# First unit of a sparse attention and gated feed-forward kernel: pair 0 by the hardware DMA queue, key maxima from PSUM, turns a pair ahead, and unit 0's VectorE work spread over its steps

## Chip, core and metric

The kernel runs on one core of a Trainium2 chip. The metric is the time of one execution on the device in microseconds, the median over runs. Before the change it is 263.07 us over 8 runs (262.12 to 263.72).

The engines: TensorE (PE in the profile, its weight loads PEld), VectorE (DVE), ScalarE (ACT), GpSimd (POOL) and SyncE (SP). POOL and SP issue the DMAs here: POOL those that convert f32 to bf16 on the way, into a software queue; SP those of the hardware queue.

## The reference

Inputs are q, k, v of shape (4 batches, 8 heads, 768 tokens, 64) in f32, and weights of a gated feed-forward layer.

```python
k_sum = k.reshape(B, H, nb, 32, D).max(axis=3)      # maximum over blocks of 32 keys, nb = 24
v_sum = v.reshape(B, H, nb, 32, D).mean(axis=3)     # mean over blocks of 32 values
scores_l = scale * q @ k^T, kept where |i - j| < 16
scores_s = scale * q @ k_sum^T + log(32)
a = softmax over [scores_l, scores_s] together
attn = a @ [v ; v_sum]
x = attn as (B*S, H*D) = (3072, 512)
g, val = x @ w_gate, x @ w_val                      # 512 -> 1536
ffn_out = (gelu(g) * val) @ w_out                   # 1536 -> 512
out = x + sigmoid(x @ w_res) * ffn_out
```

## The kernel before

**Tiling.** The work is cut into 8 units of 384 tokens (`TU`), two for each batch. A unit has an attention part and a feed-forward part. Heads go in 4 pairs: the 64 dimensions of two heads fill the 128 partitions. Tokens go in tiles of 64 queries, 6 to a unit.

**Attention of a pair.** `kW` holds, for each tile of 64 queries, 128 columns: 16 keys before the tile, its own 64, 16 after, 24 block maxima and 8 zeros. So one matmul per tile and head gives a [128 x 64] block of scores, all that the softmax needs, with the keys on the partitions. In unit 0 two matmuls first write the mask (`nmask`, 0 or -30000) into the score bank, which the scores are added to (`mask_step`); in other units the exponentials are multiplied with the 0/1 mask afterwards (`mask_part`). ScalarE takes the exponential into `P`. `vext` holds the values of the same 96 tokens, the block means in the last 32 partitions, and a column of ones, so that `av_part` gives sums and normalizer in one matmul. In unit 0 the means' part is a second matmul from `vsum` (`blocks=True`), so that the rest needn't wait for it. `av_norm` divides on VectorE into `xn`; `xt_step` turns it by TensorE and copies it on ScalarE into `xT`.

**Making kW, qT and vext.** In batch 0 tokens are loaded with 96 partitions (`load_tokens`), turned by TensorE through the identity (`turn_pair`, in PSUM buffers `mm`), and copied: `k_step` copies the keys into `kW` on ScalarE (L199), and `k_rest` on VectorE takes block maxima from there (a maximum of halves, L206; a reduce, L208), the neighbours of each tile (L210, L211) and spreads the maxima over the tiles (L212). `q_step` copies on ScalarE (L216). Values are loaded in 7 chunks (`load_values`: six of 128 tokens, the first one with 112, and a last one of 16 tokens); `v_spread` copies between halves of the tiles on VectorE; `vsum_sum` makes block means by matmuls with `bmean`, one for each chunk; `vsum_out` copies them; `vsum_bc` writes them into `vext`.

**Feed-forward.** For each of 12 steps `fo`, 4 matmuls make g and 4 make vv (`half_fo`, 128x384 each), ScalarE takes Gelu (L370), VectorE multiplies (L371) into `gvT`. Then `res_part` and `ffn_step` give the output, finished by `end_step`.

**Order.** All orders are written out by hand in the program: each engine runs its instructions in the order of the calls. During the steps `fo` of one unit the values and keys of the next batch are prepared (`values_step`, `k_step`, `k_rest`, `q_step`), and at its end the next unit's attention is interleaved with its `ffn_step`. `keep_warm(n)` puts n matmuls on zeros into TensorE's queue; there are 30 in the first unit.

**Loads.** On POOL, in this order: k and q of pairs 0 and 1, then of pairs 2 and 3 (between them the `affine_select` that makes the identity), value chunks 0 to 6 with the selects of the mask and of `bmean` between them, six pairs of weight chunks (columns for two steps fo each), q of unit 1 (`qb`), `w_res`, three chunks of `w_out`, then batch 1 (`load_batch`, called at fo 4 of unit 0). A load is given one of eight semaphores in turn, so that a load's issue waits for the landing of the eighth load before it.

The stretch ahead of unit 0's steps, and the functions that the change touches:

Of the kernel before, what the change touches and what calls it, by code (L numbers as in the profile page):

```python
# [15 lines left out]
def kernel(  # L16
# [86 lines left out]
    with tc.manual_schedule():  # L103
# [13 lines left out]
        def select(ap, op, fill, base, step, cm):  # L117
            nc.gpsimd.affine_select(out=ap, in_=ap, compare_op=op, fill=fill, base=base,
                                    pattern=[[step, ap.shape[-1]]], channel_multiplier=cm)

        def mask_consts():
            nc.vector.memset(maskt[:], 1.0)
            select(maskt[0:96], ALU.is_ge, 0.0, -1, -1, 1)
            select(maskt[0:96], ALU.is_ge, 0.0, 2 * WIN - 1, 1, -1)
            nc.vector.tensor_scalar(nmask[:], maskt[:], 30000.0, -30000.0, ALU.mult, ALU.add)

        nc.vector.memset(warm[:], 0.0)
        nc.vector.memset(ident[:], 0.0)
        nc.vector.memset(bias_t[:], 0.0)
        nc.vector.memset(bias_t[96:128, :], logblk)  # L130
        nc.vector.memset(bmean[:], 1.0 / BLK)
        vext_consts(0)

        kt, qa, qb = token_tile(0, S, "k0"), token_tile(0, TU, "qa"), token_tile(TU, S, "qb")
        k_sb[0] = kt
        load_tokens(kt, k, 0, 0, S, 0, 4)
        select(ident[:], ALU.not_equal, 1.0, 0, -1, 1)
        load_tokens(qa, q, 0, 0, TU, 0, 4)
        load_tokens(kt, k, 0, 0, S, 4, 8)
        load_tokens(qa, q, 0, 0, TU, 4, 8)  # L140
        select(bias_t[96:128, :], ALU.is_ge, -30000.0, NB - 1, 0, -1)
        load_values(0, 0)
        mask_consts()
        kw_consts(0)
        load_values(0, 1)
        select(bmean[:], ALU.is_ge, 0.0, 32 * (NB + 94) - WIN, -32, 1)
        select(bmean[:], ALU.is_ge, 0.0, 31 + WIN - 32 * (NB + 94), 32, -1)
        for c in range(2, NC + 1):
            load_values(0, c)
        nc.vector.memset(vsum[0][96:128, :, D:D + 1], 1.0)  # L150

        wg_src = moe_w_gate.rearrange("(ko ki) f -> ki ko f", ki=128)
        wv_src = moe_w_val.rearrange("(ko ki) f -> ki ko f", ki=128)
        for c in range(6):
            sl = slice(c * 256, (c + 1) * 256)
            nc.gpsimd.dma_start(out=w_gate[:, :, sl], in_=wg_src[:, :, sl])
            nc.gpsimd.dma_start(out=w_val[:, :, sl], in_=wv_src[:, :, sl])
        load_tokens(qb, q, 0, TU, S, 0, H)
        nc.gpsimd.dma_start(out=w_res[:], in_=moe_w_res.rearrange("(ko ki) f -> ki ko f", ki=128))
# [53 lines left out]

        def q_step(src, b, lo, hi, hp, pool, tag):
            tp = turn_pair(src, hp, pool, tag)
            nc.scalar.copy(qT[b % 2][hp][:, lo:hi].rearrange("d (p j) -> d p j", j=tp.shape[2]), tp)  # L216

# [29 lines left out]

        def vsum_sum(b, pool, tag, chunks=range(NC + 1), vs=None):
            if vs is None:
                vs = pool.tile([128, DM], F32, tag=tag, name="vs")  # L250
            for c in chunks:
                lo = NB - 2 - 4 * c if c < NC else 0
                rows, t = (slice(0, 128), 2 * c) if c < NC else (slice(64, 64 + WIN), NT - 1)
                nc.tensor.matmul(vs[:], bmean[rows, lo:lo + 128], vext[b % 2][rows, t, :, 0:D],  # L254
                                 start=(c == 0), stop=(c == NC), skip_group_check=True)
            return vs

        def vsum_out(b, vs, h0, h1, copy):
            copy(vsum[b % 2][96:128, h0:h1, 0:D],
                 vs[96:128, h0 * D:h1 * D].rearrange("p (h d) -> p h d", d=D))  # L260
# [14 lines left out]

        def mask_step():
            s = ps_s.tile([128, 2, 512], F32, tag="s", name="s")
            for hh in range(2):
                nc.tensor.matmul(s[:, hh, 0:TU].rearrange("p (t q) -> p t q", t=HT), ident[:],
                                 nmask.unsqueeze(1).to_broadcast([128, HT, QT]),  # L280
                                 start=True, stop=False, skip_group_check=True)
            return s

        def s_step(u, hp, st, s=None, two=None, masked=True):
            b, half = u // 2, u % 2
            first = s is not None
            if two:
                s = [pool.tile([128, 512], F32, tag=tag, name="s1") for pool, tag in two]
            elif not first:
                s = ps_s.tile([128, 2, 512], F32, tag="s", name="s")  # L290
# [126 lines left out]
        def values_step(u, fo):  # L417

            b = u // 2 + 1
            if u == 1 and fo >= 8:  # L420
                i = fo - 8
                if i == 0:
                    vs = vsum_sum(1, *SS)
                    vsum_out(1, vs, 0, H, nc.scalar.copy)
                    v_spread(1, 0, HT // 2, 0)
                if i == 1:
                    v_spread(1, 0, HT // 2, 1)
                if i in (2, 3):
                    vsum_bc(1, 2 * i - 4, 0, HT)
                    vsum_bc(1, 2 * i - 3, 0, HT)  # L430
            if u in (2, 4) and fo >= FO - NP:
                block_sums(vT[b], fo - FO + NP)
            if u in (3, 5):
                if fo in (1, 3):
                    v_spread(b, 0, HT // 2, fo // 2)
                if fo == 4:
                    vsum_turn(b, *SS)
                if 5 <= fo < 9:
                    vsum_bc(b, fo - 5, 0, HT)
            if u % 2 == 0 and u < NU - 1:  # L440
                if fo in (0, 1):
                    v_spread(b - 1, HT // 2, NC, fo)
                if fo in (2, 3):
                    vsum_bc(b - 1, 2 * fo - 4, HT, NT)
                    vsum_bc(b - 1, 2 * fo - 3, HT, NT)


        st = new_unit()
        wp = ps_o.tile([128, 512], F32, tag="ao", name="wp")
        keep_warm(13, wp)  # L450
        nc.scalar.activation(pre[:], bias_t[0:1, :], AF.Exp)
        for hp in range(2):
            k_step(0, hp, *MM)
            q_step(qa, 0, 0, TU, hp, *MM)
        s = mask_step()
        keep_warm(3, wp)
        s_step(0, 0, st, s)
        k_step(0, 2, *MM)
        q_step(qa, 0, 0, TU, 2, *MM)
        s = mask_step()  # L460
        s_step(0, 1, st, s)
        k_step(0, 3, *MM)
        q_step(qa, 0, 0, TU, 3, *MM)
        s = mask_step()
        s_step(0, 2, st, s)
        v_spread(0, 0, HT // 2, 0)
        v_spread(0, 0, HT // 2, 1)
        vs = vsum_sum(0, *MM, range(0, 3))
        keep_warm(2, wp)
        s = mask_step()  # L470
        s_step(0, 3, st, s)
        keep_warm(2, wp)
        for c in range(3, NC + 1):
            vsum_sum(0, *MM, range(c, c + 1), vs)
            keep_warm(2 if c < NC else 1, wp)
        vsum_out(0, vs, 0, 2, nc.vector.tensor_copy)
        vsum_out(0, vs, 2, 8, nc.scalar.copy)
        nc.scalar.activation(pre[:], bias_t[0:1, :], AF.Gelu)
        homes = (AO, TT, MM, MM)
        for p in (0, 2):  # L480
            for hp in (p, p + 1):
                av_part(0, hp, st, *homes[hp], blocks=False)
            for hp in (p, p + 1):
                av_part(0, hp, st, blocks=True)
                av_norm(hp, st)
        keep_warm(3)
        two = ps_s.tile([128, 2, 512], F32, tag="s", name="gv0")
        firsts = [(w_gate, 0, two[:, 0, :]), (w_val, 0, two[:, 1, :]), (w_gate, 1, None), (w_val, 1, None)]
        for hp in range(NP):
            xt_step(0, hp, st, *(TT if hp % 2 else AO), nc.scalar.copy)  # L490
            if hp:
                firsts = [(w, fo, half_fo(st, w, fo, hp - 1, hp, acc)) for w, fo, acc in firsts]

        for u in range(NU):
# [17 lines left out]
            for fo in range(FO):  # L512
# [11 lines left out]
                if u == 0 and fo == 4:  # L524
                    nc.vector.memset(vsT[:], 0.0)
                    vext_consts(1)
                    kw_consts(1)
                    load_batch(1)
                if u == 2 and fo == FO - 1:
# [9 lines left out]
                if u == 1 and fo == 6:  # L539
                    gate(gvT[0:1, fo, 0:1])  # L540
                    load_batch(2)
                if u == 1 and fo in (0, 1, 4, 5):
                    home = TT if fo % 2 else AO
                    if fo < 4:
                        k_step(nb, fo, *home)
                    else:
                        q_step(q_sb[nb], nb, 0, S, fo - 4, *home)
                if u == 1 and fo >= FO - 2:
                    k_rest(kW[1][fo - FO + NP])
                if u == 0 and fo >= FO - 2:  # L550
                    for hp in range(2 * (fo - FO + 2), 2 * (fo - FO + 2) + 2):
                        q_step(qb, 0, TU, S, hp, *(TT if hp % 2 else AO))
# [108 lines left out]
```

## Time and profile before

The profiled execution took 263.07 us, its span (first to last instruction) is 260.8 us.

| what | value |
|---|---|
| TensorE busy | 250.6 us, 96% of the span |
| VectorE, ScalarE busy | 173.4 us (66%), 130.3 us (50%) |
| g and vv matmuls (L364) | 712 listed, 0.326 us each, pipelined at about 0.16 |
| Gelu (L370), gvT product (L371) | 0.49 us, 0.55 us |
| exponential of a pair (L305) or half (L302) | 0.90 us, 0.58 us |
| kW copy (L199), qT copy of 384 (L216) | 0.80 us, 0.49 us |
| halves' maximum (L206), reduce (L208) | 0.35 us, 0.55 us |
| value chunk issue on POOL (L99) | 0.89 us |
| DMA | 29.6 MB, 113 GB/s on average, 190 to 205 GB/s in most of the first 45 us |

The page lists instructions by engine and line, with the tile written and the tiles read; a row's last part says how long its engine sat idle before it and what ended that. The granted clock is that of TensorE's throttle. A matmul's duration in a row includes the pipeline, so that the distance between starts, not the duration, is what a queue of them costs.

### The profile page before, as it was taken

How to read it: one execution, taken by the hardware profiler on the slowest of the kernel's cores; microseconds unless marked ns; L12 is line 12 of the kernel's file. 1: busy time of each engine (PE TensorE's matmuls, PEld its weight loads, DVE VectorE, ACT ScalarE, POOL GpSimd, SP SyncE). 2: the span in 40 equal slices, each digit the busy share in tenths (PEclk: the TensorE clock that was granted, in tenths of full speed). 3: DMA queues.
4: the chain of work that ended last, by engine and by line, in shares of the span. 5: the costliest groups of instructions: out<-in, count | busy, mean ns of one | idle time of the engine just before them, and what ended most of it. 6: DMA issues, size and time to landing. Idle time of an engine off the chain costs nothing.

```text
span 260.8 us, 5738 instructions
## 1 busy us (share of the span) xinstructions
PE 250.6 (96%) x2239; PEld 140.7 (54%) x2264; DVE 173.4 (66%) x414; ACT 130.3 (50%) x224; POOL 100.3 (38%) x137
## 2 busy tenths in 40 slices
PE   7789999999999999999999999999999999999995
PEld 2536554556555565555555565455645565556544
DVE  3744862576497878679966778588948754674424
ACT  2745449556375535745374535735364536443310
POOL 7966542990899910997560100010000100020000
PEclk9999999999999999999999999999999999999999
DMA  5999999999999999999993885644002200130012
GB/s 80 173 168 196 196 205 193 143 153 187 150 122 129 166 157 160 110 175 205 157 138 36 197 124 91 48 127 87 0 4 74 95 0 0 33 112 26 1 40 80
DMA packets 116746, 29.60 MB, mean 113 GB/s; under 512 B 103664, under 2 KB 114544, under 8 KB 116720
## 3 DMA queue, kind: packets, MB, share of 16 engines
q0 software_dynamic: 86992, 19.41, 84.2%
q1 hardware_dynamic: 29728, 9.84, 22.0%
q8 instruction: 17, 0.28, 0.5%
q14 instruction: 9, 0.07, 0.1%
HBM read 32.51 MB, written 6.29 MB: 149 GB/s over the span
## 4 chain that ended last, share of the span: by engine, by line
PE 84%; DVE 6%; POOL 3%; DMA 3%; issue 2%; ACT 1%; POOLq 0%; DVEq 0%
PE f L398 22%; PE vv L364 21%; PE g L364 20%; PE r L382 8%; PE ao L328 4%; DMA vext<-in_v_dram 3%; PE gv L510 3%; PE s L296 2%; DVE gvT L371 2%; POOL vext L99 2%; PE xp L347 1%; PE vs L254 1%; DVE ks L208 1%; DVE vext L274 1%; PE gv L364 1%
## 5 line engine op out<-in xcount | busy, mean ns | idle before, releaser
L364 PE MATMUL vv<-xT,w_val 128*128 128x384 bf16 x364 | 74.5, 326 | 0.2 <-DVE gvT L371 0.2
L370 ACT ACTIVATE ge<-g 128x384 f32<-128x384 f32 x87 | 42.7, 490 | 61.8 <-PE g L364 33.8
L364 PE MATMUL g<-xT,w_gate 128*128 128x384 bf16 x348 | 71.3, 326 | 0.0
L371 DVE TENSOR_TENSOR gvT<-ge,vv 128x384 bf16<-128x384 f32 x91 | 49.8, 551 | 27.9 <-PE vv L364 26.0
L398 PE MATMUL f<-w_out,gvT 128*128 128x512 bf16 (+2 forms) x298 | 66.6, 362 | 0.7
L364 PEld LDWEIGHTS <-w_val 128*128 128x128 bf16 x368 | 36.0, 98 | 24.8 <-issue 1.2
L364 PEld LDWEIGHTS <-w_gate 128*128 128x128 bf16 x352 | 33.9, 98 | 22.7 <-issue 0.7
L398 PEld LDWEIGHTS <-gvT 128*128 128x128 bf16 x312 | 28.3, 98 | 28.2
L409 POOL DMA_DIRECT2D out_dram<-o x12 | 6.5, 544 | 92.6 <-DVE rz L336 77.7
L388 ACT ACTIVATE th<-r 128x512 f32<-128x512 f32 x24 | 14.2, 602 | 25.9 <-PE r L382 25.9
L403 DVE SCALAR_TENSOR_TENSOR th<-th,f 128x512 f32<-128x512 f32 (+2 forms) x26 | 16.7, 641 | 12.3 <-PE f L398 8.5
L382 PE MATMUL r<-w_res,xT 128*128 128x512 bf16 x88 | 24.0, 380 | 0.4
L99 POOL DMA_DIRECT2D vext<-in_v_dram x28 | 23.6, 886 | 1.4 <-PE g L364 0.7
L313 DVE TENSOR_TENSOR P<-P,maskt 128x768 bf16<-128x768 bf16 x28 | 15.5, 557 | 12.5 <-ACT P L305 8.3
L172 POOL DMA_DIRECT2D k_sb<-in_k_dram x24 | 19.7, 848 | 10.2 <-DMA w_out<-in_moe_w_out_dram 5.2
L172 POOL DMA_DIRECT2D q_sb<-in_q_dram x24 | 20.0, 873 | 0.0
L338 DVE TENSOR_TENSOR xn<-ao,rz 128x384 bf16<-128x384 f32 x32 | 17.8, 557 | 1.1
L305 ACT ACTIVATE P<-s,bias_t 128x768 bf16<-128x768 f32 x18 | 16.2, 902 | 3.8 <-PE s L296 3.7
L349 ACT COPY xT<-xp 128x384 bf16<-128x384 bf16 x20 | 9.3, 480 | 17.5 <-PE xp L347 15.8
L405 DVE SCALAR_TENSOR_TENSOR o<-th,xn 128x512 f32<-128x512 f32 (+2 forms) x26 | 16.9, 651 | 0.9
L302 ACT ACTIVATE P<-s,bias_t 128x384 bf16<-128x384 f32 x28 | 14.6, 577 | 0.0
L172 POOL DMA_DIRECT2D v_sb<-in_v_dram x16 | 13.2, 866 | 2.9 <-DMA q_sb<-in_q_dram 2.9
(87 smaller groups left out, 230.7 us busy)
## 6 DMA issues: line engine op xcount, KB each, us to landing
out_dram<-o POOLq DMA_DIRECT2D x12, 256.0 KB, 2.4
out_dram<-o SPq DMA_DIRECT2D x11, 256.0 KB, 5.3
vext<-in_v_dram POOLq DMA_DIRECT2D x20, 128.0 KB, 6.9
k_sb<-in_k_dram POOLq DMA_DIRECT2D x24, 96.0 KB, 5.4
q_sb<-in_q_dram POOLq DMA_DIRECT2D x24, 96.0 KB, 4.3
w_gate<-in_moe_w_gate_dram POOLq DMA_DIRECT2D x6, 256.0 KB, 8.7
w_val<-in_moe_w_val_dram POOLq DMA_DIRECT2D x6, 256.0 KB, 8.9
w_out<-in_moe_w_out_dram POOLq DMA_DIRECT2D x3, 512.0 KB, 14.1
```

What stands on the lines that cost most here:

```text
L99: nc.gpsimd.dma_start(out=dst, in_=v[b, :, lo:hi, :].rearrange("h p d -> p h d"))
L172: nc.gpsimd.dma_start(out=sb[b][:, h // 2, :, h % 2 * D:h % 2 * D + D], in_=src[b, h].rearrange("(c p) d -> p c d", c=NC))
L305: nc.scalar.activation(P.rearrange("p a t q -> p a (t q)"), s[:, :, 0:TU], AF.Exp, scale=scale, bias=bias_t[:])
L313: nc.vector.tensor_mul(Pf, Pf, maskt.unsqueeze(1).to_broadcast([128, 2 * HT, QT]))
L338: nc.vector.tensor_mul(xn, ao[:, :, :, 0:D], rz.to_broadcast([128, NSUB, 2, D]))
L364: nc.tensor.matmul(acc[:, 0:TU], w[:, ko, fs], st["xT"][:, ko, :], start=(ko == 0), stop=(ko == KO - 1))
L370: nc.scalar.activation(ge[:], g[:, 0:TU], AF.Gelu)
L371: nc.vector.tensor_mul(gvT[:, fo, :], ge[:], vv[:, 0:TU])
L382: nc.tensor.matmul(r[:], st["xT"][:, ko, ss], w_res[:, ko, :], start=(ko == 0), stop=(ko == KO - 1))
L398: nc.tensor.matmul(st["f", sub][:, 0:c1 - c0], gvT[:, fo, ss], w_out[:, fo, c0:c1], start=(fo == 0), stop=(fo == FO - 1))
L403: nc.vector.scalar_tensor_tensor(th, th, 1.0, f[:, 0:c1 - c0], ALU.add, ALU.mult)
L405: nc.vector.scalar_tensor_tensor(o[:, 0:c1 - c0].rearrange("p (k d) -> p k d", d=128), th.rearrange("p (k d) -> p k d", d=128), 0.5, st["x ...
```

## The change

It rewrites the stretch ahead of unit 0's steps and moves work in units 0 and 1. The k and q of pair 0 come by SP as f32 (`kf`, `qf`) and are converted on ScalarE and VectorE; POOL loads the other pairs one by one. The 16-token value chunk is loaded first, the constants are made in another order, and `qb` is loaded before the last pair of weight chunks. In unit 0 `k_first` and `k_first_rest` take block maxima by one reduce out of PSUM and fill only the tiles of unit 0; `k_later` fills those of unit 1 in steps 8 to 11. Keys and queries of a pair are turned before the scores of the pair before it; pairs 1 and 3 have their scores in two single banks. The matmuls of `av_part` without block means stand ahead of the last sums of means; Gelu's table is loaded after the last exponential. 18 matmuls on zeros are left of 30.

```diff
@@ loads and constants
-        load_tokens(kt, k, 0, 0, S, 0, 4)
+        kf = qk.tile([PP, 2, 8 * D], F32, tag="k_sb", name="kf")
+        qf = qk.tile([PP, 2, 4 * D], F32, tag="q_sb", name="qf")
+        nc.sync.dma_start(out=kf[:], in_=k[0, 0:2].rearrange("h (p j) d -> p h (j d)", j=8))
+        nc.sync.dma_start(out=qf[:], in_=q[0, 0:2, 0:TU].rearrange("h (p j) d -> p h (j d)", j=4))
+        load_tokens(kt, k, 0, 0, S, 2, 4)
         select(ident[:], ALU.not_equal, 1.0, 0, -1, 1)
-        load_tokens(qa, q, 0, 0, TU, 0, 4)
-        load_tokens(kt, k, 0, 0, S, 4, 8)
-        load_tokens(qa, q, 0, 0, TU, 4, 8)
+        load_tokens(qa, q, 0, 0, TU, 2, 4)
+        for h in (4, 6):
+            load_tokens(kt, k, 0, 0, S, h, h + 2)
+            load_tokens(qa, q, 0, 0, TU, h, h + 2)
+        select(maskt[0:96], ALU.is_ge, 0.0, -1, -1, 1)
+        select(maskt[0:96], ALU.is_ge, 0.0, 2 * WIN - 1, 1, -1)
+        load_values(0, NC)
+        load_values(0, 0)
         select(bias_t[96:128, :], ALU.is_ge, -30000.0, NB - 1, 0, -1)
...
+        for c in range(1, NC):
+            load_values(0, c)
         select(bmean[:], ALU.is_ge, 0.0, 32 * (NB + 94) - WIN, -32, 1)
         select(bmean[:], ALU.is_ge, 0.0, 31 + WIN - 32 * (NB + 94), 32, -1)
...
         for c in range(6):
             sl = slice(c * 256, (c + 1) * 256)
+            if c == 5:
+                load_tokens(qb, q, 0, TU, S, 0, H)
...
@@ keys of unit 0
+        def k_first(hp):
+            tp = ps_mm.tile([128, 8, PP], BF16, tag="mm", name="tp")
+            for j in range(8):
+                for hh in range(2):
+                    nc.tensor.transpose(tp[hh * 64:hh * 64 + 64, j, :], kt[:, 2 * hp + hh, j, :], ident[0:PP, 0:PP])
+            kw = kW[0][hp]
+            nc.scalar.copy(kw[:, :, OWN:OWN + QT].rearrange("d t (p j) -> d t p j", j=8),
+                           tp.rearrange("d j (t p) -> d t p j", t=NT))
+            return tp, kw
+
+        def k_first_rest(tp, kw):
+            ks = work.tile([128, NB], BF16, tag="ks", name="ks")
+            nc.vector.tensor_reduce(out=ks[:], in_=tp.rearrange("d j (n w) -> d n j w", w=4),
+                                    axis=mybir.AxisListType.XY, op=ALU.max)
+            nc.vector.tensor_copy(kw[:, 0:HT, BLK0:BLK0 + NB], ks.unsqueeze(1).to_broadcast([128, HT, NB]))
+            nc.vector.tensor_copy(kw[:, 1:HT, 0:WIN], kw[:, 0:HT - 1, OWN + QT - WIN:OWN + QT])
+            nc.vector.tensor_copy(kw[:, 0:HT, POST:POST + WIN], kw[:, 1:HT + 1, OWN:OWN + WIN])
+
+        def k_later(kw):
+            nc.vector.tensor_copy(kw[:, HT:NT, 0:WIN], kw[:, HT - 1:NT - 1, OWN + QT - WIN:OWN + QT])
+            nc.vector.tensor_copy(kw[:, HT:NT - 1, POST:POST + WIN], kw[:, HT + 1:NT, OWN:OWN + WIN])
+            nc.vector.tensor_copy(kw[:, HT:NT, BLK0:BLK0 + NB], kw[:, 0:HT, BLK0:BLK0 + NB])
@@ the stretch ahead of unit 0's steps
+        s1 = s_tiles((AO, TT))
+        keep_warm(8, s1[0])
+        nc.scalar.copy(kt[:, 0].rearrange("p j d -> p (j d)"), kf[:, 0])
+        nc.vector.tensor_copy(kt[:, 1].rearrange("p j d -> p (j d)"), kf[:, 1])
+        nc.vector.tensor_copy(qa[:, 0:2].rearrange("p h j d -> p h (j d)"), qf[:])
+        t = k_first(0)
+        q_step(qa, 0, 0, TU, 0, *MM, nc.vector.tensor_copy)
+        nc.vector.tensor_scalar(nmask[:], maskt[:], 30000.0, -30000.0, ALU.mult, ALU.add)
+        k_first_rest(*t)
+        t = k_first(1)
+        q_step(qa, 0, 0, TU, 1, *MM)
+        k_first_rest(*t)
+        s = mask_into(s_tiles())
+        keep_warm(2, s1[0])
+        s_step(0, 0, st, s)
+        keep_warm(2, s1[0])
+        mask_into(s1)
+        t = k_first(2)
+        q_step(qa, 0, 0, TU, 2, *MM)
+        k_first_rest(*t)
+        s_step(0, 1, st, s1, True)
+        s = mask_into(s_tiles())
+        t = k_first(3)
+        q_step(qa, 0, 0, TU, 3, *MM, nc.vector.tensor_copy)
+        k_first_rest(*t)
+        vs = ps_mm.tile([128, DM], F32, tag="mm", name="vs")
+        keep_warm(1, vs)
+        s_step(0, 2, st, s)
+        s3 = mask_into(s_tiles((AO, TT)))
+        wp = ps_mm.tile([128, 512], F32, tag="mm", name="wp")
+        vsum_sum(0, *MM, (NC, 0), vs)
+        keep_warm(2, wp)
+        s_step(0, 3, st, s3, True)
+        nc.scalar.activation(pre[:], bias_t[0:1, :], AF.Gelu)
         v_spread(0, 0, HT // 2, 0)
         v_spread(0, 0, HT // 2, 1)
-        vs = vsum_sum(0, *MM, range(0, 3))
+        vsum_sum(0, *MM, (1, 2, 3), vs, first=False)
         keep_warm(2, wp)
...
+        homes = (MM, MM, AO, TT)
+        for hp in range(2):
+            av_part(0, hp, st, *homes[hp], blocks=False)
+        vsum_sum(0, *MM, (4,), vs, first=False)
+        for hp in range(2, NP):
+            av_part(0, hp, st, *homes[hp], blocks=False)
+        keep_warm(1, wp)
+        vsum_sum(0, *MM, (5,), vs, first=False, last=True)
         vsum_out(0, vs, 0, 2, nc.vector.tensor_copy)
         vsum_out(0, vs, 2, 8, nc.scalar.copy)
+        for hp in range(NP):
+            av_part(0, hp, st, blocks=True)
+            av_norm(hp, st)
-        keep_warm(3)
...
@@ units 0 and 1
-                if fo in (2, 3):
-                    vsum_bc(b - 1, 2 * fo - 4, HT, NT)
-                    vsum_bc(b - 1, 2 * fo - 3, HT, NT)
+                if 2 <= fo < 2 + NP:
+                    vsum_bc(b - 1, fo - 2, HT, NT)
...
                 if u == 0 and fo == 4:
                     nc.vector.memset(vsT[:], 0.0)
+                    load_rows(1)
+                if u == 0 and fo == 6:
                     vext_consts(1)
+                if u == 0 and fo == FO - 1:
                     kw_consts(1)
-                    load_batch(1)
+                    for c in range(NC + 1):
+                        load_values(1, c)
-                if u == 1 and fo in (0, 1, 4, 5):
+                if u == 1 and fo in (1, 2, 6, 7):
...
-                if u == 1 and fo >= FO - 2:
-                    k_rest(kW[1][fo - FO + NP])
-                if u == 0 and fo >= FO - 2:
-                    for hp in range(2 * (fo - FO + 2), 2 * (fo - FO + 2) + 2):
+                if u == 1 and fo in (8, 9):
+                    k_rest(kW[1][fo - 6])
+                if u == 0 and fo >= FO - 4:
+                    k_later(kW[0][fo - FO + 4])
+                if u == 0 and fo in (FO - 3, FO - 2):
+                    for hp in range(2 * (fo - FO + 3), 2 * (fo - FO + 3) + 2):
```

In unit 1's `values_step`, the sums of block means (`vsum_sum`, `vsum_out`) and the first `v_spread` move from fo 8 to fo 10, and the second `v_spread` and all four `vsum_bc` to fo 11.

## The prediction

> **What bounds the kernel now.** I read the windows table first, then the chain of waits, then the timeline of the stretches that these single out. Columns of the windows: stretch, its length, busy time of each engine with its count of instructions, granted clock, DMA share, GB/s.
>
> ```profile
> 5.00:10.00 5.00, 3.65 (x71) 2.04 (x71) 3.12 (x21) 2.36 (x4) 4.81 (x9) 1.00 1.32 191
> 10.00:15.00 5.00, 3.87 (x82) 2.41 (x82) 3.03 (x13) 4.65 (x7) 4.75 (x7) 1.00 2.89 150
> 15.00:20.00 5.00, 4.45 (x33) 1.69 (x33) 1.94 (x6) 1.08 (x3) 2.87 (x4) 1.00 1.78 180
> 20.00:25.00 5.00, 4.44 (x117) 3.43 (x118) 2.73 (x8) 3.20 (x6) 3.47 (x6) 1.00 1.45 197
> 25.00:30.00 5.00, 5.00 (x34) 3.03 (x33) 2.97 (x6) 2.40 (x6) 2.85 (x5) 1.00 1.45 196
> ```
>
> From 25 us on TensorE is full, and the page has it 96% busy over 260.8 us. So a gain must come from the first 25 us, or from a stall later. Much of the early busy time is warm-up matmuls on zeros. The chain in that window names what really ends last:
>
> ```profile
> 6.17 0.83 POOL vext L99
> 7.71 2.57 POOL vext L99 x3
> 10.27 8.09 DMA vext<-in_v_dram
> 19.91 2.07 PE ao L328 x96
> ```
>
> The value chunk issued at 9.4 lands at 17.4, the next at 18.4; until then nothing that needs the block means can start. The timeline shows what follows:
>
> ```profile
> 18.40 0.38 PE L254 MATMUL vs<-vext,bmean 128*128 128x512 bf16 x1 [0.16 <-DMA vext<-in_v_dram]
> ...
> 19.47 0.39 PE L415 MATMUL wp<-warm 128*128 128x512 bf16 x1
> 19.91 0.57 PE L328 MATMUL ao<-vext,P 96*64 96x65 bf16 x24
> ```
>
> All 96 ao matmuls queue behind the last vs sum, so the first reciprocal comes at 20.83, then four norms at 0.69 each:
>
> ```profile
> 20.83 0.20 DVE L336 RECIPROCAL rz<-ao 128x6 f32<-128x6 f32 x1 [0.96 <-PE ao L328]
> ...
> 23.14 0.56 DVE L338 TENSOR_TENSOR xn<-ao,rz 128x384 bf16<-128x384 f32 x1
> ```
>
> The last quarter of fo 0 then starts at 25.83, and full feed-forward work at 26.5. Two later stalls:
>
> ```profile
> 41.71 0.33 PE L296 MATMUL s<-qT,kW 64*128 64x64 bf16 x11 [0.20 <-ACT qT L216]
> ...
> 78.89 0.85 PE L328 MATMUL ao<-vext,P 128*64 128x65 bf16 x24 [0.24 <-DVE P L313]
> ```
>
> At unit 0's end the 24 score matmuls took 40.86 to 41.98, 1.12 us; at unit 1's end 73.70 to 74.16, 0.46. The difference, 0.66, is the late q copies. At 78.48 the r matmuls end, ao starts at 78.89 and takes 0.78 where 0.50 is usual: 0.69 lost to late masks.
>
> **The change, step by step (us after the span's start).**
>
> *Pair 0 by the hardware queue.* SP is free at 0.8, so kf is issued at about 0.9, qf 0.3 later (an SP issue takes 0.33). The nearest row is SP's output writes: 1.6 to landing at best, and 256 KB alone moved in 0.85 after 0.9 of latency. kf (384 KB in f32) then lands near 3.2, qf near 3.7. Bounds: 2.5, and 5.9 if it took the 5.0 that the first k load by POOL took. Up to 4.1 it costs nothing: VectorE's constants end at 3.59 now, plus twelve kW memsets (0.4, as at 34.3) gives 4.1. Then its two casts; no row shows an f32 cast from SBUF; between 0.30 (32x128 cast) and 0.70 (64x1536 copy) I take 0.45: 5.0. ScalarE's cast (0.60, as the 128x512 tanh) is beside it. TensorE is in its 8 warm-up matmuls (0.43 each) until 4.7.
>
> *Pair 0 to scores.* k turns (0.53) to 5.25, q turns (0.36) to 5.6, kW copy on ScalarE (0.80) to 6.05, qT copy on VectorE to 6.1. Here stands a new wait: nmask now queues on VectorE behind these and ahead of the maxima, and waits for maskt, whose selects stand on POOL behind six token loads (about 0.6 to 0.7 each from 1.4): 6.2. With nmask (0.78 before) 6.9. The maxima: one 128x768 reduce (0.95, as the vsT reduce) to 7.9, three copies 0.5 to 8.4. Scores at 8.45, against 9.68 now.
>
> *Pairs 1 to 3.* The maxima read PSUM, but in the changed program the reduce still waits for ScalarE's copy of the same tile. So ScalarE's order rules: P0 8.85 to 9.75, kW2 to 10.95, qT2 to 11.45, P1 as two halves (2 x 0.52) to 12.5, kW3 13.3; reduce and copies to 14.75; scores 3 at 14.8, P3 done at 16.25 (now 16.85). k and q of pair 3, last landing at 11.2 now, come in a queue relieved of pair 0's 288 KB (1.5 us at the 191 GB/s of the window): 10, in time for the turns at 11.
>
> *Values.* v_spread runs 14.75 to 16.15 on VectorE (0.70 each), then ao without blocks for pairs 0 and 1, vs 4, pairs 2 and 3, a warm-up, vs 5: 17.9. The last value chunk is issued near 11.3 and, without the two to three us [...], lands near 14.5; with that lag 17: either way in time. vsum 18.25, blocks, first reciprocal near 18.6 (now 20.83). VectorE's norms end at 21.5; turns, copies and first quarters fit between, no three warm-up matmuls stand ahead, and fo 0's last quarter starts at 22.4 instead of 25.83: 3.4 gained. Gelu's table load (1.28) moves to 16.3 to 17.6, covered by the vs sums; were they earlier it would hold vsum's copy, at most 1.
>
> *Unit 0.* k_later's twelve copies (about 0.15 each), vsum_bc singly and the constants at fo 4, 6, 11 keep gvT in step: the bunched memsets at 32.3 to 34.6 now cost 0.26 (nine steps of 1.30 from 26.48 make fo 9 35.58; it starts at 35.84). qb is turned a step earlier: 0.66. Unit 1: k_rest a step or two earlier, vs at fo 10: VectorE gets vs's 1.7 to catch up, masks end before r does: 0.65.
>
> *What the weight stream allows.* Weights are issued after bmean, near 12.9, data from 14.5; at 1.32 per 256 KB (the spacing of landings now) and qb (2.0) ahead of chunk 5, its w_val lands between 32.7 and 34.9. It is needed at 37.79 less 3.7 plus the moved q turns, 34.6: nothing to 0.3. Batch 1's last values land at 67.3 now, 0.7 before vs; the stream gains some 1.0, vs moves to 67.96 + 2.6 - 4.3 = 66.3: up to 0.5 lost, I take 0.3.
>
> *Two rules against this change.* (1) L211 took 0.60 and L212 0.56 at 8.9, where POOL was issuing:
>
> ```profile
> 8.86 0.60 DVE L211 COPY kW<-kW 128x176 bf16<-128x176 bf16 x1
> ...
> 10.41 0.19 DVE L211 COPY kW<-kW 128x176 bf16<-128x176 bf16 x1
> ```
>
> The Trainium skill, "GPSIMD Engine Reference", Key points, says that GpSimd shares its SBUF interfaces with VectorE and that VectorE's two-port modes contend. POOL now issues without pause to 12.9. By the rule each pair's copies pay 0.4, of which two pairs lie on the path: gain 0.8 less. By the row, two of four copies under POOL paid nothing; I take 0.2. (2) The warm-up: loads of warm come each 0.43 to 4.66, then four in 0.75, so the array went to full speed after 3.4 us of matmuls. The skill, "TensorE: Matmul & The Clock Gate", Part 1, says that the window is free-running and that an idle window halves the clock. 8 matmuls last just 3.4. By the rule the release may slip past 4.7; the granted clock of 1.00 in every window says that it doesn't here. Price below.
>
> Sum: 3.4 + 0.26 + 0.66 + 0.65 = 5.0, less 0.2 (contention) and 0.3 (batch 1's values): 4.5. The profiled execution is 263.07 (span 260.8, 2.3 around it), which is the median of the eight runs: 258.6.
>
> **Rivals.**
> - *The DMA stream takes it back.* The weights' head start is only about 1 us, since POOL issues them later. If one engine lags longer, chunk 5 or batch 1's values stop TensorE until the stream comes: with their slack now (4.0 less 2.0 for qb plus 0.5; 0.7 plus 2.6 for the two moved steps), the gain ends near 2 to 3: 260.6. For: the DMA is saturated to 67 us. Against: all weights have 4 us in hand now.
> - *The front is no faster.* Casts, nmask and ScalarE's order are all new waits ahead of v_spread; if they add 3 us (a late kf, 5.9, adds 1.8; contention 1.2), norms start as now and only the later stalls are won: 1.2 less 0.5, 262.3, hardly the same.
> - *Slower: the clock gate.* Twelve of 30 warm-up matmuls go (18 stay), and the turns that fill the front may not count: the same page, Part 4, says so of transposes. No row here shows it. If the array is at half clock from 5 us and released only by unit 0's dense work, its part of the front's path (some 4 us) doubles and 3.4 to 6.8 us of unit 0 run at half speed, 1.7 to 3.4 lost: 6 to 7 against 4.5, 265. It decides from 4.5 us lost, that is if the release comes after about 23 us.
>
> **How the numbers follow.** 0.3% (0.8 us) is about what a measurement of this kernel can tell from no change. Main case 0.66 (258.6, from 257.4 to 260), stream 0.17 (260.6), front no faster 0.07 (262.3), clock 0.10 (265). Faster takes the first two and a part of the third: 0.86; same 0.05; slower 0.09. The range leaves out the clock case and the worst of the third.
>
> **What would show it.** Right: the first norm near 18.6, fo 0's last quarter near 22.4, scores 0 near 8.45, no ACT wait at unit 0's end and no mask wait at unit 1's, as many feed-forward matmuls as now. Wrong: kf landing after 4.1; maxima waiting on ScalarE past 14; L396 waiting for a weight DMA; vs of batch 1 waiting for vext; 128x384 matmuls 0.32 apart instead of 0.16 in unit 0.

## The result and the profile after

The changed kernel takes 261.81 us (median of 19 runs, 259.55 to 264.58), beside 262.89 us for the kernel before (56 runs). The ratio is 0.9942, 95% interval 0.9924 to 0.996, so about 1.5 us are gained where 4.5 were forecast. 261.81 lies above the forecast range. Ratios and intervals leave out disturbed runs (over 1.5% above the kernel's fastest), so that ratio and median differ where these are many: 8 of 12 with the sum of means at step 8, the profiled execution among them, 5 of 22 with a step of unit 2 twice, 3 of 12 with only the new first unit.

The profiled execution took 260.77 us, 2.3 less than the one before. So this profile shows one of the better executions of the changed kernel. From 15 to 25 us, in the windows table (stretch, length, busy time of PE, PEld, DVE, ACT, POOL with counts, granted clock, DMA share, GB/s):

```profile
15.00:20.00 5.00, 4.14 (x103) 2.47 (x102) 2.47 (x6) 2.96 (x5) 4.97 (x8) 1.00 1.40 167
20.00:25.00 5.00, 4.65 (x37) 2.94 (x36) 2.57 (x8) 3.00 (x7) 2.60 (x4) 1.00 1.43 192
```

TensorE's gaps end within 20 to 25 us (4.65 busy, 4.44 before), and POOL now issues without pause to 20 us (4.97 busy from 15 to 20, 2.87 before). The timeline of the front, on two engines:

```profile
4.51 0.42 DVE L481 CAST k<-kf 96x512 bf16<-96x512 f32 x1 [0.27 <-DMA kf<-in_k_dram]
8.23 0.35 PE L328 MATMUL s<-qT,kW 64*128 64x64 bf16 x12
14.58 0.35 PE L328 MATMUL s<-qT,kW 64*128 64x64 bf16 x12 [0.39 <-DVE kW L237]
18.41 0.30 DVE L286 CAST vsum<-vs 32x128 bf16<-32x128 f32 x1 [2.00 <-PE vs L281]
19.18 0.20 DVE L368 RECIPROCAL rz<-ao 128x6 f32<-128x6 f32 x1 [0.46 <-PE ao L360]
23.29 0.32 PE L396 MATMUL gv<-xT,w_gate 128*128 128x384 bf16 x1
```

The scores of pair 0 start at 8.23 (9.68 before), those of pair 3 at 14.58, the first norm at 19.18 (20.83). The last quarter of fo 0 starts at 23.29 (25.83): the first unit is 2.5 us earlier. Unit 0's end no longer waits for q copies; its 24 score matmuls go through in 0.45 us where they took 1.12:

```profile
38.20 0.52 PE L328 MATMUL s<-qT,kW 64*128 64x64 bf16 x24
38.65 0.39 PE L414 MATMUL r<-w_res,xT 128*128 128x512 bf16 x1
```

There the kernel stands 3.3 us ahead. The timeline of unit 1's last two steps shows where it is given back, the sum of means of the kernel before first:

```profile
67.96 1.80 PE L254 MATMUL vs<-vext,bmean 128*128 128x512 bf16 x7
```

```profile
67.24 1.26 PE L281 MATMUL vs<-vext,bmean 128*128 128x512 bf16 x5
69.49 0.83 PE L281 MATMUL vs<-vext,bmean 128*128 128x512 bf16 x2 [0.99 <-DMA vext<-in_v_dram]
...
77.05 0.85 PE L360 MATMUL ao<-vext,P 128*64 128x65 bf16 x24 [0.44 <-DVE P L345]
```

The sum of means stands one step before the end now, starts at 67.24 and waits 0.99 us for the values of batch 1. What VectorE makes from it is late by that, so the masks delay ao by 0.44 us again. The chain of waits names what came last (start, length, what):

```profile
30.23 15.31 DMA w_out<-in_moe_w_out_dram
...
45.82 0.82 POOL k_sb L174
...
46.66 5.39 POOL q_sb L174 x7
...
53.21 4.60 POOL vext L99 x6
...
58.34 11.56 DMA vext<-in_v_dram
...
69.95 0.37 PE vs L281
```

From 30 to 70 us no instruction of TensorE is in this chain. It is POOL's queue: the weights' landings release the issue of the last keys, eight query loads of 0.8 us each follow, then the values, and the last of these takes 11.6 us to land. In the kernel before, the same stretch of its chain was TensorE but for 0.9 us of two q copies at unit 0's end. Milestones of the profiled executions:

| start of | before, us | after, us | ahead, us |
|---|---|---|---|
| scores of pair 0 | 9.68 | 8.23 | 1.45 |
| last quarter of fo 0 | 25.83 | 23.29 | 2.54 |
| r matmuls at unit 0's end | 41.98 | 38.65 | 3.33 |
| unit 1's first g matmul | 54.92 | 51.60 | 3.32 |
| unit 2's first g matmul | 87.47 | 85.62 | 1.85 |
| end of the span | 260.8 | 258.9 | 1.9 |

From unit 2 on, both kernels take 173.3 us. So everything was decided before 86 us, and unit 1 took back 1.5 us.

### The profile page after: what moved, and what is told of

It reads as the page before. It is cut to its first block, busy times and chain, and to the rows that moved or that the text cites. A ratio compares the mean times of both kernels' runs of the same rounds, so it can differ in the third digit from the quotient of the medians.

```text
span 258.9 us, 5732 instructions
## 1 busy us (share of the span) xinstructions
PE 247.9 (96%) x2227; PEld 139.1 (54%) x2252; DVE 178.2 (69%) x426; ACT 130.6 (50%) x225; POOL 100.8 (39%) x139
## 4 chain that ended last, share of the span: by engine, by line
PE 69%; DMA 14%; POOL 11%; DVE 3%; issue 2%; POOLq 0%; DVEq 0%
PE f L430 20%; PE vv L396 17%; PE g L396 16%; PE r L414 7%; DMA w_out<-in_moe_w_out_dram 6%; DMA vext<-in_v_dram 4%; DMA w_gate<-in_moe_w_gate_dram 4%; POOL vext L99 4%; PE gv L552 3%; POOL q_sb L174 2%; PE ao L360 2%; PE s L328 2%; POOL w_gate L159 1%; POOL w_val L160 1%; POOL k L90 1%
## 5 line engine op out<-in xcount | busy, mean ns | idle before, releaser
L334 ACT ACTIVATE P<-s,bias_t 128x384 bf16<-128x384 f32 x32 | 16.7, 578 | 1.3 <-PE s L328 1.3
L337 ACT ACTIVATE P<-s,bias_t 128x768 bf16<-128x768 f32 x16 | 14.4, 900 | 2.9 <-PE s L328 2.8
```

The lines of the kernel that those rows point to most:

```text
L334: nc.scalar.activation(P[:, hh].rearrange("p t q -> p (t q)"), s[hh][:, 0:TU], AF.Exp, scale=scale, bias=bias_t[:])
```

## The experiments

Two theories. DATA: the stream of loads into batch 1 ends at a time of its own, and unit 1 waits for it, so a first unit that is earlier brings nothing. The rivals: CLOCK, fewer warm-up matmuls cost a part of the gain; FRONT, the gain is lost on the engines, within units 0 and 1.

**The changed kernel again.**

> The changed kernel again, beside the others on one chip. Both theories: 1.5 us (0.6%) faster than before. Theory DATA (batch 1's value chunks and turned keys set the end of unit 1, whatever the first unit does): in the profile the first unit ends 3.3 us earlier than before, the sum of block means in unit 1 waits 1 us or more for vext, and 1.9 are left after unit 1. Theory CLOCK (the array is sometimes released late): runs differ by about 1.7 us for each window of 3.4 us at half clock, and the mean granted clock of each run says which.

261.3 us (12 runs, one of them at 325.6 with a mean granted clock of 0.75), ratio 0.9915 (0.9885 to 0.9944): 2.2 us gained by this ratio. The waits of TensorE from 20 to 90 us in this profile:

```profile
PE vs L281 <- DMA vext<-in_v_dram: 1.7, 1, 1.7
PE vv L396 <- DMA w_val<-in_moe_w_val_dram: 0.5, 1, 0.5
PE g L396 <- DMA w_gate<-in_moe_w_gate_dram: 0.4, 1, 0.4
```

Its last quarter of fo 0 was 0.5 us earlier than in the first profile, but the weights of the last two steps were late by 0.9 us and the values by 1.7. (A fourth row, 0.4 us for a norm, is left out; it is the same in every kernel with the new first unit.) What is waited for differs from execution to execution.

**Eleven warm-up matmuls.**

```diff
-        keep_warm(8, s1[0])
+        keep_warm(11, s1[0])
```

> 11 warm-up matmuls ahead of the first turn instead of 8. Theory CLOCK: 8 end at 4.7 us, before the array is released, and in some runs the release slips by one or two windows of 3.4 us; with 11 the mean granted clock is 0.997 or more in every run, none is at 0.986 to 0.993, and the median is 0.6 to 0.9 us below the changed kernel's. Theory DATA alone: the clock is not what costs, and the median stays within 0.3 us of the changed kernel's, as unit 1 waits anyway.

260.93 us (6 runs), ratio 0.9911 (0.9883 to 0.994), beside 0.9915 on the same chip for the kernel with 8. The interval doesn't tell the two apart, and three of six executions still had a mean clock of 0.990 to 0.993: more warm-up is no cure. It doesn't show that the clock costs nothing (last section). The run says something else too: its first unit is 0.95 us later (scores of pair 0 at 9.17, the last quarter of fo 0 at 24.24), and the time is no longer; in its profile nothing waits for the values.

**A step of unit 0 twice, and the same in unit 2.** The second pass of 8 matmuls adds 1.3 us of TensorE.

```diff
+                elif u == 0 and fo == 5:
+                    g, vv = half_fo(st, w_gate, fo, 0, KO), half_fo(st, w_val, fo, 0, KO)
+                    half_fo(st, w_gate, fo, 0, KO, g)
+                    half_fo(st, w_val, fo, 0, KO, vv)
+                    fo_end(gvT, fo, g, vv)
```

> Step 5 of unit 0 does its 8 feed-forward matmuls twice (same result): 1.30 us more for TensorE in unit 0. Theory DATA: the wait in unit 1 shrinks by as much, since the values land no later; 0 to 0.4 us slower than the changed kernel. If instead TensorE's own work bounds unit 1 and the wait seen was a chance of one execution, it is 1.2 to 1.4 us slower.

> The control to the doubled step of unit 0: the same 8 matmuls twice in step 5 of unit 2, behind the wait for batch 1's values. Both theories: 1.2 to 1.4 us slower than the changed kernel (262.6 where that is 261.3), since nothing in unit 2 takes it back. If this too costs nothing, the doubled step says nothing on unit 1's wait.

In unit 0: 261.17 us (18 runs), ratio 0.9926 (0.9906 to 0.9947), between the two ratios of the changed kernel (0.9942 and 0.9915). In unit 2: 262.72 us (22 runs), ratio 0.9971 (0.9946 to 0.9995), 0.8 to 1.5 us more than these two. So 1.3 us of the scarcest engine cost nothing that can be told from noise ahead of unit 1's sum of means, and about their full price behind it. In the profile of the first one the sum starts at 68.76 and no row of TensorE's waits names the values: the last of them landed at 67.4, where the changed kernel's landed at 69.9. DATA had expected them no earlier.

**Unit 1's sum of means back at step 8.**

```diff
-            if u == 1 and fo == FO - 2:
+            if u == 1 and fo == FO - 4:
                 vs = vsum_sum(1, *SS, last=True)
```

> Unit 1's sum of block means (and its copy and first v_spread) back at step 8, as before; everything else as changed. Theory DATA: the values land at a time that the first unit doesn't move, so the sum ends no earlier than 70 us, and steps 9 and 10 (2.6 us), which hid part of the wait, now come behind it: 2 to 2.6 us slower than the changed kernel, as slow as the kernel before. If the wait is only a short delay of one transfer, 0 to 0.5 us slower.

264.85 us (12 runs), ratio 0.9932 (0.9892 to 0.9973). The ratio rests on four executions and is the changed kernel's own, so the 2 to 2.6 us that DATA expected are not shown. The profile, an execution of 264.16 us, shows the wait chunk by chunk:

```profile
64.64 0.82 PE L281 MATMUL vs<-vext,bmean 128*128 128x512 bf16 x3
66.21 0.38 PE L281 MATMUL vs<-vext,bmean 128*128 128x512 bf16 x1 [0.75 <-DMA vext<-in_v_dram]
67.28 0.38 PE L281 MATMUL vs<-vext,bmean 128*128 128x512 bf16 x1 [0.69 <-DMA vext<-in_v_dram]
69.34 0.38 PE L281 MATMUL vs<-vext,bmean 128*128 128x512 bf16 x1 [1.68 <-DMA vext<-in_v_dram]
69.89 0.37 PE L281 MATMUL vs<-vext,bmean 16*128 16x512 bf16 x1 [0.18 <-DMA vext<-in_v_dram]
```

The sum starts 2.6 us earlier than in the changed kernel and ends at the same time, 70.26 against 70.32; TensorE follows the chunks as they land (3.3 us of waits). Right behind, from 71.14 to 74.55 us, the granted clock is 0.50 (last section). Whether the move to step 10 gained time by itself is not shown; in this profile step 10 hides more of the wait than step 8.

**Only the changes to units 0 and 1** (the first unit, with its loads, is that of the kernel before; `qb` ahead of weight chunk 5, batch 1's loads and constants at fo 4, 6 and 11, turns, masks and sum of means as in the change).

> The kernel before, with only the changes in units 0 and 1 (constants spread over steps, qb a step earlier and ahead of the last weight chunks, keys and queries of batch 1 turned a step or two later, sum of block means at step 10, k_rest at 8 and 9); the first unit as before. Theory DATA: values land at 67.3, and the sum now starts near 69.7, so nothing waits; the two stalls of 0.66 and 0.65 go: 1.2 to 1.5 us faster than before, nearly as much as the whole change, since unit 1's wait takes the rest. If the first unit's gain counts in full, the whole change should be 2.5 us faster than this.

261.2 us (12 runs), ratio 0.9942 (0.9917 to 0.9968): as fast as the whole change. The sum starts at 69.19 and waits for nothing; the last values landed at 68.4.

**Only the new first unit** (those hunks undone in the changed kernel).

> The changed kernel with only the new first unit; the work of units 0 and 1 (loads of batch 1, turns of q and k, masks, sum of means at step 8, second part of q behind all weights) stands as before. DATA: sum of means at step 8 comes at about 62 to 65 and waits for the values, which land near 67 to 70 as the queue's order sets them: 262.3 to 263.2, nothing gained. FRONT: the 2.5 us that the first unit is earlier remain: 260 to 261.

262.93 us (12 runs), ratio 0.9975 (0.9943 to 1.0008): 0.7 us by the ratio, at most 1.5, and the interval includes no change. In its profile the sum of means waited 0.8 us for values and ended at 70.16. That execution also lost 1.7 us by the clock at 22 us (last section), so the wait alone doesn't explain its time; the ratio carries the verdict.

**Four query loads less.** The queries of heads 4 to 7 of batch 1 aren't loaded, and the turns of pairs 2 and 3 read heads 0 to 3. No instruction of TensorE, VectorE or ScalarE changes; four loads go from the queue ahead of the values. The kernel so leaves out half of batch 1's queries and serves only for timing. The edit was put into three kernels, on another chip than most runs with all loads; each ratio is to the kernel before on its own chip.

```diff
-                for h in range(H) if b > 1 else (4, 5, 6, 7, 0, 1, 2, 3):
+                for h in range(H) if b > 1 else range(4) if sb is q_sb else (4, 5, 6, 7, 0, 1, 2, 3):
...
-                    in_=q_sb[b][:, hp].rearrange("p c d -> p (c d)"))
+                    in_=q_sb[b][:, hp - 2 if b == 1 else hp].rearrange("p c d -> p (c d)"))
```

> The changed kernel, with the queries of heads 4 to 7 of batch 1 not loaded (pairs 2 and 3 of batch 1 are turned from heads 0 to 3 instead): four loads of about 0.8 us each leave the stream ahead of batch 1's values, no instruction of TensorE changes. DATA (the values of batch 1 set the end of unit 1, so the first unit's gain is absorbed there): the values land some 2 to 3 us earlier, near 67, unit 1's sum of means waits for nothing, and the time falls by 1 to 2 us to 259.5 to 260.5. FRONT (the gain of the first unit is lost elsewhere, in unit 1 or by clock): 261.3 to 261.8, as the changed kernel.

> The same queries left out in the kernel before. There the values arrived 0.7 us ahead of the sum of means, so both DATA and FRONT expect no change: 262.5 to 263.2. A gain of 1 us or more would say that the shorter stream pays by itself (fewer transfers beside the work), and the comparison with the changed kernel would have to be corrected by it.

> The kernel before with only the changes to units 0 and 1, and the same queries left out. DATA: its first unit is as late as before, so the values are in time here with little in hand, and it gains at most 0.5: 260.7 to 261.3; the difference to the changed kernel with the same edit, 0.7 to 1.7, is what the new first unit is worth when no transfer holds it. FRONT: the two stay equal within 0.5.

| median, us (runs); ratio to the kernel before | all loads | four loads less |
|---|---|---|
| kernel before | 262.87 (23 runs) | 262.74 (12); 0.9978 |
| units 0 and 1 only | 261.2 (12); 0.9942 | 261.03 (6); 0.9916 |
| changed kernel | 261.81 (19); 0.9942 and 261.3 (12); 0.9915 | 258.90 (5); 0.983 (0.9801 to 0.9859) |

The changed kernel gains 2.4 to 2.9 us by it (2.2 to 2.9 by the ratios); the other two gain 0.1 and 0.2 (0.6 and 0.7 by the ratios). So most of it is not the shorter stream by itself: it pays where the first unit is early. With it the new first unit is worth 261.03 - 258.90 = 2.1 us; with all loads the whole change and units 0 and 1 alone differ by no more than noise. The five runs also lie closer together (258.32 to 259.42). POOL's timeline of the changed kernel and then of this one:

```profile
46.66 6.55 POOL L174 DMA_DIRECT2D q_sb<-in_q_dram  x8
53.14 5.80 POOL L99 DMA_DIRECT2D vext<-in_v_dram  x7
```

```profile
46.84 1.64 POOL L174 DMA_DIRECT2D q_sb<-in_q_dram  x2
...
50.90 5.74 POOL L99 DMA_DIRECT2D vext<-in_v_dram  x7
```

The values start 2.2 us earlier and the last of them lands at 64.5, 5.4 earlier. The sum of means is one block without a wait, ended at 69.24 instead of 70.32:

```profile
67.44 1.80 PE L281 MATMUL vs<-vext,bmean 128*128 128x512 bf16 x7
```

This execution reaches unit 2's first g at 83.75, 3.7 us ahead of the kernel before.

**Batch 1's values ahead of its queries.**

```diff
                 if u == 0 and fo == 4:
-                    load_rows(1)
+                    load_rows(1, 0)
                 if u == 0 and fo == 6:
                     vext_consts(1)
+                    for c in range(NC + 1):
+                        load_values(1, c)
+                    load_rows(1, 1)
                 if u == 0 and fo == FO - 1:
                     kw_consts(1)
-                    for c in range(NC + 1):
-                        load_values(1, c)
...
-                turn_batch(1, 2, NP)
+                turn_batch(1, 2, NP, 1)
+                turn_batch(1, 2, NP, 2)
```

`load_rows(1, 0)` loads the keys, `(1, 1)` the queries; the last argument of `turn_batch` picks the turns of keys (1) or queries (2), which SP now issues in that order. Queries are loaded from head 0 on instead of head 4.

> Batch 1's loads in another order: keys, then the seven value chunks, then the queries (heads 0 to 7), and the turns of keys of pairs 2 and 3 by DMA ahead of those of queries. Theory DATA: values land some 5 us earlier, unit 1's sum of means doesn't wait, and it is 1.2 to 1.6 us faster than the changed kernel. If the whole of batch 1's traffic is the bound rather than its order, the wait moves to the queries of pair 0 in step 6, and the gain is under 0.5 us. Theory CLOCK alone: no change.

259.83 us (6 runs), ratio 0.9883 (0.9852 to 0.9914). All loads are there, only their order differs. The waits of TensorE from 20 to 90 us:

```profile
PE vv L397 <- DMA w_val<-in_moe_w_val_dram: 0.4, 1, 0.4
PE xp L380 <- DVE xn L371: 0.4, 1, 0.4
PE tp L187 <- DMA q_sb<-in_q_dram: 0.2, 1, 0.2
PE g L397 <- DMA w_gate<-in_moe_w_gate_dram: 0.2, 1, 0.2
```

The values are gone from the list. The xn row is the front's norms, as in the changed kernel. The weights of the last steps take 0.6 us, between the two profiles of the changed kernel (none and 0.9); 0.2 for queries is new.

**The same, with `qb` in halves:** heads 0 to 3 ahead of weight chunk 5, heads 4 to 7 behind it.

> Values ahead of queries in batch 1, as in the run that had it, and qb in two halves: heads 0 to 3 ahead of the last pair of weight chunks, heads 4 to 7 behind it. Theory DATA for unit 0: the last weight chunk lands about 1 us earlier, the two waits for it in step 10 (0.6 us together with values first, 0.9 in the changed kernel) go, and it is 0.3 to 0.6 us faster than with values first alone (259.8). If the second half of qb lands too late for its turn after step 10, or the waits were rare, no gain.

259.81 us (5 runs), ratio 0.9874 (0.9835 to 0.9913). The weight waits are gone from the profile, the time is the same within the interval. Both kernels beat the changed one by 1.5 to 2 us and the one before by 3 (medians).

**Two theories against the runs.** DATA holds in what costs the time: take the values out of the way, by fewer loads or by their order, and the gain of the first unit appears. FRONT does not: the first unit is 2.5 us earlier in the profile, and its gain stands when the values are in time. But DATA's picture of a stream that ends at a time of its own is wrong, as the next section shows. CLOCK is left open as a smaller, second loss.

## Why the prediction was wrong

Term by term, from the profiled executions of the changed kernel and of the same with four loads less, each against the one of before.

| step | forecast | changed kernel | four loads less |
|---|---|---|---|
| front, to fo 0's last quarter | +3.4 | +2.5 | +2.5 |
| VectorE's bunched work in unit 0 | +0.26 | +0.1 | 0.0 |
| q copies at unit 0's end | +0.66 | +0.67 | +0.66 |
| unit 1 (masks, less the wait for values) | +0.65 - 0.3 | -1.5 | +0.6 |
| contention | -0.2 | in the front | in the front |
| sum | 4.5 | 1.85 | 3.7 |

**The failed step** is "Batch 1's last values land at 67.3 now, 0.7 before vs; the stream gains some 1.0, ... up to 0.5 lost, I take 0.3". The stream gained only 0.36: the last key load is issued at 45.82 instead of 46.18, since POOL issues the first weights at 12.88, later than the 11.73 of before, and only then runs on without the wait that it had there. And the last values landed at 69.9 in the profile, 2.6 later instead of 1.0 earlier, though they were issued 0.37 earlier: the time from issue to landing, which the text took as it was, grew from 8.6 to 11.6 us. In unit 1 this cost 1.5 us where 0.35 were to be gained. The last two value chunks, before first, then after (the smaller figure is the last chunk's):

```profile
DMA to landing us min/median/max: 8.6/9.0/9.3
```

```profile
DMA to landing us min/median/max: 11.6/11.8/12.0
```

The windows of the two in between:

```profile
59.00:61.00 2.00, 2.00 (x15) 1.22 (x13) 1.97 (x9) 1.07 (x3) 0.32 (x1) 1.00 1.81 221
```

```profile
59.00:61.00 2.00, 2.00 (x14) 1.21 (x13) 1.15 (x3) 0.57 (x2) 0.00 (x0) 1.00 1.86 57
```

The rate (last column) falls from 221 to 57 GB/s, with POOL's issues over and the values in flight; packets that began between 58 and 59 us took up to 2.3 us. SP's transfers are in flight there too: unit 0's output writes, then the turns of batch 1's keys and queries. They start when unit 0 ends, so the earlier first unit brought them ahead of the values (SP's issues, before, after, and after with the doubled step of unit 0):

```profile
54.84 2.98 SPq L409 DMA_DIRECT2D out_dram<-o  x3
```

```profile
51.52 2.98 SPq L441 DMA_DIRECT2D out_dram<-o  x3
```

```profile
53.04 2.98 SPq L441 DMA_DIRECT2D out_dram<-o  x3
```

All profiles with the values behind the queries but two, one execution each, ordered by how long SP's writes start ahead of the values:

| kernel | SP's writes start | first value issued | first lands after | last value lands | sum of means waits |
|---|---|---|---|---|---|
| changed kernel again | 52.09 | 54.37 | 8.0 us | 71.1 | 1.7 |
| changed kernel | 51.52 | 53.14 | 8.7 us | 69.9 | 1.0 |
| eleven warm-up matmuls | 52.44 | 53.68 | 6.7 us | 68.3 | none |
| step of unit 0 twice | 53.04 | 53.43 | 5.6 us | 67.4 | none |
| only the new first unit | 53.94 | 54.00 | 7.7 us | 69.8 | 0.8 |
| units 0 and 1 only | 53.47 | 53.42 | 6.9 us | 68.4 | none |
| four loads less | 51.71 | 50.90 | 4.7 us | 64.5 | none |
| kernel before | 54.84 | 53.51 | 4.9 us | 67.3 | none |

The two left out are the changed kernel's own program up to this point (sum of means at step 8, step of unit 2 twice): 8.6 and 8.4 us, landed at 69.8 and 71.2. First values that are issued 0.8 us or more ahead of SP's writes land after 4.7 and 4.9 us, the others after 5.6 to 8.7. With the doubled step only TensorE's work changed, unit 0 ended 1.5 us later, and the last value landed 2.5 us earlier. So in these profiles the arrival does follow the first unit, and on the whole the wrong way round: the earlier it ends, the later the values. That SP's traffic is the cause, and which part of it, is not shown, since no run held it back alone, and the rows are not in perfect order. What is shown by times is that fewer or later loads ahead of the values bring the gain out.

Unit 1's masks did what was forecast (0.6 us in the kernel with four loads less), but in the changed kernel a late sum of means brought a mask wait back, 0.44 us. In the sum the two were added as if they were independent; both hang on the same landing.

**The front** was over-sized by 0.9. kf landed at 4.51, not 3.2, past the limit of 4.1 that the text named (the rows it was sized by are writes near the program's end, with no load beside them; kf had four of POOL's beside it); still pair 0's scores came 0.2 earlier than forecast. That is luck: the turns came 0.5 late and `nmask` took 0.27 instead of the 0.78 allowed for it. Then the small terms: the copy of `vsum` for heads 0 and 1 ended at 18.71 (18.25 forecast) and the first norm came 0.47 behind it (0.35 forecast), so the norms run from 19.18 to 22.05, 0.55 late. The last 0.35 is TensorE's order: each pair's turn stands behind four quarter matmuls of the pair before, which the text let fit between.

**Right:** the q copies (0.67 for 0.66), the scores of pairs 0 and 3, ScalarE's order as what the maxima wait for (1.13 us ahead of pair 2's reduce), the same number of feed-forward matmuls. The two rules weighed: (1) VectorE's copies while POOL issued took 0.62 (L235 at 8.98) and 0.45 (at 11.77), but 0.20 at 13.79, also during an issue, against 0.22 at 7.68: as in the rows of before, some pay and some don't. (2) The text takes a granted clock of 1.00 in every window as a sign that the release doesn't slip. That reading fails: the kernel with eleven warm-up matmuls shows 1.00 from 1.30 to 4.70 us too, while its weight loads for warm-up stand 0.43 us apart up to 5.08, twice as far as later. In the changed kernel the cost was small: the first turns took 0.64 us instead of 0.53. A slip of the text without effect: the nine steps from 26.48 to 35.58 are seven.

**The rivals:** "the DMA stream takes it back" is what happened, by batch 1's values above all and chunk 5's weights in some executions. It was given 0.17 and a gain of 2 to 3 us; the measured one was 1.5 by the first ratio and 2.2 by the second. The argument against it, "all weights have 4 us in hand now", spoke of the weights, while the values had 0.7.

## What to carry to other kernels

A gain ahead of a point that waits for a queue of loads is worth no more than the queue's slack there: look for the first consumer behind the gain whose loads the gain doesn't move, and cap the sum of all stages ahead of it by that slack before adding those behind. Then ask which other transfers the gain does move, and whether they now run ahead of these loads: here the slack (0.7 us and the two moved steps, 2.6) would nearly have been enough, had the values still landed at 67.3. To see whether such a point is there, add known work ahead of it and behind it: here 1.3 us were free in unit 0 and cost 0.8 to 1.5 in unit 2. Then order the loads by the time of their first use; values ahead of queries brought back what the faster first unit had lost.

## What the runs showed of the hardware

- An issue on POOL of a load of batch 1 (96 or 128 KB) took 0.82 us; 15 of them back to back held the queue for 12 us (46.66 to 58.94), so that the last values were issued no earlier, however idle their consumer.
- Loads of POOL's queue that stood behind SP's writes and turns took up to 8.7 us to land where 4.9 were enough ahead of them (table above; the cause is not separated).
- The granted clock can fall right after a stretch in which TensorE has no long gap. In the profile of the kernel with only the new first unit it was 0.50 from 21.3 to 24.7 us, where the matmuls of fo 0 are 0.32 us apart instead of 0.16:

```profile
17.90:21.30 3.40, 2.52 (x58) 1.62 (x59) 2.27 (x7) 1.10 (x3) 2.48 (x4) 1.00 1.30 163
21.30:24.70 3.40, 3.40 (x17) 2.00 (x15) 0.77 (x3) 1.29 (x3) 1.92 (x3) 0.50 1.45 197
```

  That costs 1.7 us (half of 3.4). In the profile with the sum of means at step 8 the same comes after the wait for the values:

```profile
67.73:71.14 3.41, 1.63 (x8) 0.69 (x8) 0.20 (x2) 0.66 (x2) 2.31 (x3) 1.00 2.59 144
71.14:74.55 3.41, 3.41 (x13) 1.65 (x11) 1.79 (x6) 0.90 (x2) 2.46 (x4) 0.50 2.41 150
```

  Two more profiles have such a stretch: values first with `qb` in halves (8.12 to 11.53, the 3.41 us ahead busy for 1.72) and the kernel before with four loads less (13.36 to 16.77, busy for 2.06 ahead). The Trainium skill, "TensorE: Matmul & The Clock Gate", Part 1, says that the gate closes after an idle window of some 3.4 us; the length agrees, but the windows ahead were not idle, they were busy for 1.6 to 2.5 us by the profile. Cut into windows of 3.41 us from its own first change of clock, the changed kernel's profile is busy for 2.7 to 2.9 in each from 5.45 to 22.5 us and keeps full clock; but it kept it too after a window from 66.89 that was busy for 2.34, so these traces give no threshold.
- How often it falls differs between the kernels: the mean clock is 0.984 to 0.994 in 12 of 31 executions of the changed kernel (without the one at 325.6 us), and 0.992 to 0.994 in 16 of 91 of the kernel before; over all kernels, in 53 of 117 with the new first unit and 20 of 121 with the old one. At 1.7 us for each such stretch that is some 0.4 us of the changed kernel's gain, an estimate from the first two counts; its median is 1.1 us higher in such executions. So the clock rival is real, if small beside the 3 us missing, and three more warm-up matmuls didn't mend it.
- A transfer by SP at the program's start was slow: kf (384 KB) was issued at 0.82 and landed at 4.51, 3.7 us later; SP's output writes at the program's end, 64 KB, had 1.6. Size and the loads beside it differ too, so the start alone is not shown as the cause.
